# A retention block and two fused MLPs in float32: order of one chunk load, pacing of weight loads, and place of one pair's block sums

## The chip, the cores and the metric

The kernel runs on one core of one Trainium2 chip. Five engines of that core take part: TensorE (PE, with its weight loads on PEld), VectorE (DVE), ScalarE (ACT), and SyncE (SP), whose queue issues nearly all transfers; GpSimd is idle. The metric is device time in microseconds, the median of several executions.

## The reference

```
scores = q @ k.T / sqrt(64);  ret = scores * gamma_h ** (i - j) for i >= j, else 0;  a = ret @ v
x  = a, heads side by side                     # 2304 tokens x 512 (4 sequences of 576, 8 heads of 64)
x1 = softplus(x @ moe_w_in)   @ moe_w_out      # 512 -> 2048 -> 512
y  = relu(x1 @ moe2_w_in)**2  @ moe2_w_out     # 512 -> 2048 -> 512
```

All of it is float32. The kernel splits each operand into a high and a low part (fp32r) and makes three products of them (high x high, high x low, low x high).

## The kernel before

**Retention.** Tokens are handled in chunks of 128 (two halves of 64), 18 in all. The first four come from tiles of their own. From chunk 4 on, a chunk's q, k, v and a second k lie in one of two slots of `ring`; `load_chunk(c)` fills a slot with two transfers of 512 KB on SP's queue, first q and k (line 397, `ring<-in_qk_t_dram`), then k and v (`ring<-in_kv_dram`). Chunks c-1 and c+1 use the same slot. `visit(c, s)` issues the small matmuls of a half: outputs of chunk c-1 (L474), scores of chunk c (L426, which read q and k), states (L451). Then `masked` (L436, DVE) empties the scores, and `rest()`, called later in the same step, scales the outputs into x (`scaled`, L497 or L505). For tokens from 1280 on, `scaled` also stores x to `x1d` (L500). After the visit with s = 1 `rest()` ended with `load_chunk(c + 1)`.

**First MLP, tiles.** The first 1280 tokens go in three tiles b = 0, 1, 2 of 512, 384, 384 tokens. Each has 16 steps f, one per block of 128 hidden units. A step issues `g1` (L558, 12 matmuls), ACT's softplus (L569), the visits that are due (`attend`), the split of the step before (`split_g`: ACT L576, DVE L577), `rest()`, and `g2` of the step before last (L592, 12 matmuls). Visits run until step f = 5 of the last tile, one a step. All of this is issued in the order in which it is written.

**Second layer's weights.** Weights come packed; `load_w` (L141 for w_in, L146 for w_out) brings one raw block of 512 KB into one of three `stage` buffers, and `words` joins it into a `ct` tile with two ACT operations (L170, L171) and one or two DVE operations (L176, L179). `split_s` and `split_o` join two such blocks, form block sums for a Strassen-like product, split them (ACT L232, DVE L233) and store them to `s2d` or `o2d` (L235). One such item takes nine calls of `pump_step`: four for the two joins and five for the sums and stores. `pace(goal)` calls `pump_step` at the end of a step until the goal is reached. In the tiles b = 1 and 2 a step also stores a quarter of one group of w_out to `wod` (L1577), for six groups that are to be overwritten and reloaded later (`reload`, L1122).

**First MLP, full block.** The other 1024 tokens go through `block_first` (Strassen-like products `full_product`, L1015, pair p of hidden blocks after pair) and `block_second` (L1148). Their operands are made in the last tile: `load_full` brings x back (L939, into `ring`), `sums_full` and `build_full` make `t1` (L969, L718), and for pair 0 `words_of_pair` (L979) and `make_s` (L987, L996, L718) make the weight side `s`. The second MLP (`second_phase`, L697, and `second_products`, L770) follows. From `block_first` on, the order of instructions is a planner's.

Of the kernel before, what the change touches and what calls it, by code (L numbers as in the profile page):

```python
# [16 lines left out]
P = 128  # L17
# [4 lines left out]
STAGES = 3  # L22
# [13 lines left out]
A11, A12, S2, S4, S3, S1, A22 = range(7)  # L36
PRODUCTS = (A11, S2, A12, S3, S1, A22, S4)
T_SLOTS = 8
T_GROUPS = (0, 2, 3, 4)
S_GROUP = 5  # L40
G_GROUP = 1
ITEM = 9
SIGNED = 9
S_SLOTS = 10
# [10 lines left out]
def kernel(  # L55
# [70 lines left out]
    KH = KD // 2  # L126

    x1d = dram.tile([2 * FULL // CN, P, KD * CN], F32, name="x1d")
    wod = dram.tile([S_GROUP + 1, P, 4 * DM], F32, name="wod")
    s2d = dram.tile([NP, 7, P, 2, KH * P], F32, name="s2d")  # L130
    o2d = dram.tile([NP, 7, P, 2, KH * P], F32, name="o2d")

# [14 lines left out]
        staged[kind, f] = t  # L147

    last_softplus = []

    def words(t, ct):

        y, up, low = t.bitcast(F32)[:, :, 1], t[:, :, 1], t[:, :, 0]  # L160
        halves = t.bitcast(U16).rearrange("p a (b two) -> p a b two", two=2)
        half = halves[:, :, 0, 1]
        signed = n_split[0] - n_one > SIGNED
        if signed:
            with tc.issue_after(last_softplus[0].ins):
                nc.scalar.activation(
                    out=y, in_=y, func=AF.Prelu, scale=2.0**-112, alpha=-(2.0**32)
                )
        else:
            nc.scalar.activation(out=y, in_=y, func=AF.Copy, scale=2.0**-112)  # L170
        nc.scalar.activation(  # L171
            out=low, in_=half, func=AF.Identity, bias=round_up, scale=7.0 / 65535
        )
        yield
        if not signed:
            nc.vector.scalar_tensor_tensor(  # L176
                out=y, in0=y, scalar=-(2.0**32), in1=y, op0=ALU.mult, op1=ALU.max
            )
        nc.vector.scalar_tensor_tensor(  # L179
            out=ct, in0=up, scalar=3, in1=low,  # L180
            op0=ALU.logical_shift_left, op1=ALU.bitwise_or,
        )
        yield

    def new_ct(dtype=U32):
# [54 lines left out]
    def split_s(p):  # L240

        cts = []
        for f in (p, p + NP):
            t = staged.pop(("wi", f))
            cts.append(new_ct())
            yield from words(t, cts[-1])
        pump_load(n_used[0] + STAGES)
        top, bot = (ct.bitcast(F32) for ct in cts)
        a11, a12 = top[:, :KH * P], top[:, KH * P:]
        a21, a22 = bot[:, :KH * P], bot[:, KH * P:]  # L250
        store_s(s2d, p, A11, top)
        yield
        store_s(s2d, p, A22, a22)
        yield

        nc.vector.tensor_tensor(out=a22, in0=a21, in1=a22, op=ALU.add)
        nc.vector.tensor_tensor(out=a21, in0=a11, in1=a21, op=ALU.subtract)
        nc.vector.tensor_tensor(out=a11, in0=a22, in1=a11, op=ALU.subtract)
        nc.vector.tensor_tensor(out=a12, in0=a12, in1=a11, op=ALU.subtract)
        yield  # L260
        store_s(s2d, p, S3, bot)
        yield
        store_s(s2d, p, S2, top)
        yield True


    def split_o(p):

        cts = []
        for f in (p, p + NP):  # L270
            t = staged.pop(("wo", f))
            cts.append(new_ct())
            yield from words(t, cts[-1])
        pump_load(n_used[0] + STAGES)
        top, bot = (ct.bitcast(F32) for ct in cts)
        a11, a21 = top[:, :KH * P], top[:, KH * P:]
        a12, a22 = bot[:, :KH * P], bot[:, KH * P:]
        store_s(o2d, p, 0, a11)
        yield
        store_s(o2d, p, 1, bot)  # L280
        yield

        nc.vector.tensor_tensor(out=a22, in0=a21, in1=a22, op=ALU.add)
        nc.vector.tensor_tensor(out=a21, in0=a11, in1=a21, op=ALU.subtract)
        nc.vector.tensor_tensor(out=a11, in0=a22, in1=a11, op=ALU.subtract)
        nc.vector.tensor_tensor(out=a12, in0=a12, in1=a11, op=ALU.subtract)
        yield
        store_s(o2d, p, 3, top)
        yield
        store_s(o2d, p, 5, bot)  # L290
        yield True
# [30 lines left out]
    def pump_step():  # L322

        if not splitting:
            m = n_split[0]
            if m == len(items):
                return
            count, make, args = items[m]
            pump_load(n_used[0] + count)
            splitting.append(make(*args))  # L330
            n_split[0] += 1
            n_used[0] += count
        if next(splitting[0]):
            splitting.clear()
            pump_load(n_used[0] + STAGES)

    def pump(count):

# [607 lines left out]
    def sums_full(k):  # L946

        r00, r01, r10, r11 = (full_raw(i, j) for i in range(2) for j in range(2))
        if k == 1:
            full["t2"] = group_tile(G_GROUP, [P, 4 * DM], F32, "t2")[:, :KB]  # L950
            minus(r00, r01, r00)
            minus(full["t2"], r11, r00)
        elif k == 3:
            minus(r10, r10, full["t2"])
            minus(r01, r11, r01)
# [168 lines left out]
    def block_second():  # L1124

        accs = [
            [ps_acc.tile([P, 512], F32, tag="at", name="acc") for _ in range(KD)],
            [
                pool.tile([P, 512], F32, tag=tag, name="acc")
                for pool, tag in (  # L1130
                    (ps_h, f"h{n_h[0] % 2}"), (ps_h, f"h{(n_h[0] + 1) % 2}"),
                    (ps_at, "at"), (ps_st, "st"),
                )
            ],
        ]
        for g in (0, 4, 5):
            reload(g)
        split_full(2)
        for u, (f, half) in enumerate(f_units):
            at, second = divmod(u, 2)  # L1140
            begin, end = at == 0, at == KF - 1
            split_full(u + AHEAD)
            h, l = f_pairs.pop(u)
            wh, wl = of_group(f)
            for j in range(KD):
                c = slice(j * P, (j + 1) * P)
                for m, (a, x) in enumerate(((wh, h), (wh, l), (wl, h))):
                    nc.tensor.matmul(  # L1148
                        accs[half][j], lhsT=a[:, c], rhs=x,
                        start=(begin and m == 0), stop=(end and m == 2),  # L1150
                    )
            if end:
                for j in range(KD):
                    t0 = BLOCK + half * FULL
                    drain_one(j, accs[half][j], x2d[j, :, t0:t0 + FULL], FULL)
            pace(PACE[3] + (PACE[4] - PACE[3]) * (u + 1) // 26)
            if second:
                if at == 5:
                    for g in (1, 2, 3):
                        reload(g)  # L1160
                if at == 8:
                    mem["s"] = xs.tile([P, 4, 2, KH * P], F32R, tag="xr", name="sring")
                    load_s(4)
                m = {7: 0, 8: 1, 10: 2, 11: 3, 12: 4, 13: 5, 14: 6}.get(at)
                if m is not None:
                    build_t(m)
        assert n_split[0] == len(items) and not splitting
# [312 lines left out]
    def visit(c, s):  # L1480
# [11 lines left out]
        if s == 0:  # L1492
            if old:
                then.update(at_rounds((0, states(c - 1, 1))))
            rounds(first, then)
        else:
            if new:
                then.update(at_rounds((0, states(c, 0))))
            rounds(then, first)
        if new:  # L1500
            masked(c, 1 - s, pb)

        def rest():
            if s == 0 and old:
                next_state(c - 1, 1)
            elif s and new:
                next_state(c, 0)
            if old:
                scaled(c - 1, s, po)
            if s == 0:  # L1510
                scale_v(c)
            else:
                if old:
                    del chunk[c - 1]
                    load_chunk(c + 1)
        return rest


# [21 lines left out]
            return lambda: drain(t0, n)  # L1540

    n_taken = [0]

    def step(j):
        b, f = steps[j]
# [23 lines left out]
            load_chunk(last + 1)  # L1569
        if done:  # L1570
            done()
        if b:
            pace(PACE[b - 1] + (PACE[b] - PACE[b - 1]) * max(f - 1, 0) // (KF - 2))
        g, i = divmod((b - 1) * KF + f, 4)
        if 0 <= g <= S_GROUP:
            words_out = wo_group[g].rearrange("p a b n -> p (a b) n").bitcast(F32)
            nc.sync.dma_start(out=wod[g][:, i * DM:(i + 1) * DM], in_=words_out[:, i])  # L1577
        if b == last_b:
# [3 lines left out]
                build_full(BUILD_AT.index(f))  # L1582
            if f in SUMS_AT:
                sums_full(SUMS_AT[f])
            if f == KF - 3:
                words_of_pair(0)
            if f == KF - 2:
                made = make_s(0)
                next(made)
                next(made)  # L1590
                full["s0"] = made
            if ends:
                for _ in range(3):
                    next(full["s0"])

    def run(j0, j1):
        for j in range(j0, j1):
# [87 lines left out]
```

## Time and profile before

| | |
|---|---|
| median of 3 runs | 844.51 us (844.33 to 844.76) |
| profiled execution | 842.79 us, span 841.0 us |
| PE busy | 809.7 us (96%) |
| PEld busy | 717.8 us (85%) |
| DVE busy | 654.0 us (78%) |
| ACT busy | 402.3 us (48%) |
| DMA | 201.97 MB, mean 240 GB/s |
| mean granted TensorE clock | 0.991 of full speed |

The span runs from the first to the last instruction of the profiled execution. The share of PE is high, but matmuls are pipelined and their ends are modelled, so what counts is where PE sat idle, and behind what. "Clock" is the TensorE clock that was granted as a share of 2.4 GHz; 0.5 is the level of 1.2 GHz.

### The profile page before, as it was taken

To read this page: it belongs to the slowest core of one execution; us is meant where nothing else is said; L and a number is where in the kernel's file an instruction comes from. 1 tells how busy PE (TensorE), PEld (TensorE's weight loads), DVE (VectorE), ACT (ScalarE), POOL (GpSimd) and SP (SyncE) were. 2 spreads that over 40 slices of the span, in tenths; PEclk is the share of its full clock that TensorE was granted. 3 is DMA by queue.
4 is the path that set the end of the run, shared out by engine and by line. 5 is a ranking of instruction groups with operands and counts; after the bars stand their busy time and mean duration, and the time that the engine had idled before them with its cause. 6 is when DMAs were issued, how large, how long until landed. Compare 5 with 4: busy or idle time off the path is not lost.

```text
span 841.0 us, 16335 instructions
## 1 busy us (share of the span) xinstructions
PE 809.7 (96%) x5909; PEld 717.8 (85%) x5909; DVE 654.0 (78%) x1255; ACT 402.3 (48%) x781; POOL 0.2 (0%) x4
## 2 busy tenths in 40 slices
PE   8899999978799989999999999999999999999998
PEld 5678889967689978888888899988999988999887
DVE  4899885654635788996778788989698997787876
ACT  3888773543333665565657521355321554111453
POOL 0000000000000000000000000000000000000000
PEclk9999999999989999999999999999999999999999
DMA  9757664787766854335899988898988788878785
GB/s 243 261 179 235 216 213 178 252 287 245 235 204 197 248 178 148 101 113 200 303 327 281 311 289 252 251 302 270 301 257 251 247 262 281 289 251 248 254 273 172
DMA packets 129747, 201.97 MB, mean 240 GB/s; under 512 B 11010, under 2 KB 73090, under 8 KB 128898
## 3 DMA queue, kind: packets, MB, share of 16 engines
q1 hardware_dynamic: 129504, 200.85, 74.7%
q8 instruction: 47, 0.77, 0.4%
q14 instruction: 32, 0.26, 0.1%
q10 hardware_dynamic: 164, 0.09, 0.1%
HBM read 153.71 MB, written 47.19 MB: 239 GB/s over the span
## 4 chain that ended last, share of the span: by engine, by line
PE 84%; DMA 8%; DVE 4%; ACT 2%; SPq 1%; issue 1%; DVEq 0%; ACTq 0%
PE acc L592 11%; PE acc L1148 10%; PE ph L558 9%; PE py L697 9%; PE py L770 9%; PE px L697 6%; PE pz L770 6%; PE px L770 6%; PE pz L697 6%; PE py L1015 3%; DMA ring<-in_qk_t_dram 3%; PE pz L1015 2%; PE px L1015 2%; PE po L474 1%; PE pb L426 1%; DMA qk<-in_qk_t_dram 1%
## 5 line engine op out<-in xcount | busy, mean ns | idle before, releaser
L592 PE MATMUL acc<-gh,wo 128*128 128x384 f32 (+1 forms) x384 | 119.3, 372 | 0.0
L697 PE MATMUL py<-t,sring 128*128 128x384 f32 x432 | 88.3, 338 | 0.8 <-DVE uring L901 0.8
L558 PE MATMUL ph<-xh,wi 128*128 128x384 f32 (+1 forms) x376 | 79.8, 353 | 2.8 <-DVE ring L436 1.4
L592 PEld LDWEIGHTS acc<-gh,wo 128*128 128x128 f32 x384 | 73.6, 195 | 7.5 <-ACT gh L576 0.4
L697 PEld LDWEIGHTS py<-t,sring 128*128 128x128 f32 x432 | 74.8, 188 | 3.4 <-DVE uring L901 1.6
L558 PEld LDWEIGHTS ph<-xh,wi 128*128 128x128 f32 x376 | 67.3, 188 | 8.6 <-issue 1.7
L592 PE MATMUL acc<-gl,wo 128*128 128x384 f32 (+1 forms) x192 | 70.3, 366 | 1.3 <-DVE gl L577 1.3
L718 DVE TENSOR_TENSOR gring<-g,gring 128x384 fp32r<-128x384 f32 (+1 forms) x100 | 57.4, 578 | 14.1 <-ACT gring L750 9.2
L750 ACT CAST gh<-g 128x384 fp32r<-128x384 f32 x84 | 43.1, 514 | 47.5 <-PE px L770 16.7
L718 DVE TENSOR_TENSOR gl<-g,gh 128x384 fp32r<-128x384 f32 (+1 forms) x100 | 57.7, 578 | 10.1 <-ACT gh L750 8.0
L750 ACT CAST gring<-g 128x384 fp32r<-128x384 f32 x84 | 43.1, 514 | 40.3 <-PE py L770 16.4
L436 DVE TENSOR_TENSOR ring<-pb,cst 64x256 f32<-64x256 f32 x56 | 23.6, 421 | 48.1 <-PE pb L426 32.8
L697 PE MATMUL pz<-t,sring 128*128 128x384 f32 x288 | 58.9, 334 | 0.0
L697 PE MATMUL px<-t,sring 128*128 128x384 f32 x288 | 58.3, 335 | 0.0
L569 ACT ACTIVATE e<-ph 128x384 f32<-128x384 f32 (+1 forms) x48 | 25.2, 525 | 69.0 <-PE ph L558 68.7
L718 DVE TENSOR_TENSOR g<-g 128x384 f32<-128x384 f32 x96 | 52.6, 555 | 1.4
L897 ACT COPY uring<-px 128x384 f32<-128x384 f32 x24 | 11.6, 481 | 87.6 <-PE px L697 87.6
L232 ACT CAST ct<-ct 128x512 fp32r<-128x512 f32 (+1 forms) x64 | 35.9, 565 | 34.2 <-DMA s2d<-ct 16.9
L697 PEld LDWEIGHTS px<-t,sring 128*128 128x128 f32 x288 | 50.5, 188 | 0.6 <-ACT uring L897 0.5
L697 PEld LDWEIGHTS pz<-t,sring 128*128 128x128 f32 x288 | 50.8, 188 | 0.0
L233 DVE TENSOR_TENSOR ct<-ct 128x512 fp32r<-128x512 f32 (+1 forms) x64 | 39.2, 621 | 13.8 <-ACT ct L232 9.3
L1148 PE MATMUL acc<-gring,wo 128*128 128x512 f32 x192 | 44.8, 389 | 0.0
(155 smaller groups left out, 1753.4 us busy)
## 6 DMA issues: line engine op xcount, KB each, us to landing
sring<-s2d SPq DMA_DIRECT2D x168, 256.0 KB, 3.2
sring<-o2d SPq DMA_DIRECT2D x168, 256.0 KB, 3.4
wi_raw<-in_moe_w_in_dram SPq DMA_DIRECT2D x32, 512.0 KB, 5.9
wo_raw<-in_moe_w_out_dram SPq DMA_DIRECT2D x32, 512.0 KB, 4.4
s2d<-ct SPq DMA_DIRECT2D x48, 256.0 KB, 2.8
o2d<-ct SPq DMA_DIRECT2D x48, 256.0 KB, 3.2
ring<-in_qk_t_dram SPq DMA_DIRECT2D x14, 512.0 KB, 5.2
ring<-in_kv_dram SPq DMA_DIRECT2D x14, 512.0 KB, 6.1
```

What stands on the lines that cost most here:

```text
L232: nc.scalar.copy(h, src)
L233: nc.vector.tensor_tensor(out=l, in0=src, in1=h, op=ALU.subtract)
L436: nc.vector.tensor_tensor(out=chunk[c][rows, 1, i * HH:(i + 1) * HH], in0=pb[of], in1=mask[of], op=ALU.mult)
L558: nc.tensor.matmul(ph[:, :n], lhsT=a, rhs=x, start=(j == 0), stop=(j == len(todo) - 1))
L569: nc.scalar.activation(out=g, in_=hps.pop(key)[:, :n], func=AF.Softplus)
L592: nc.tensor.matmul(acc[j][:, :n], lhsT=a, rhs=x, start=(begin and m == 0), stop=(end and m == 2))
L697: nc.tensor.matmul(ps, lhsT=a, rhs=x, start=(first and m == 0), stop=(m == len(todo) - 1), skip_group_check=True,)
L718: nc.vector.tensor_tensor(out=out, in0=a, in1=b, op=ALU.subtract)
L750: nc.scalar.copy(h, src)
L770: nc.tensor.matmul(blocks[m][:, :cols], lhsT=a[:, c], rhs=x, start=(first and p == n == 0), stop=(p == NP - 1 and n == len(todo) - 1), ski ...
L1015: nc.tensor.matmul(ps, lhsT=a, rhs=x, start=(first and m == 0), stop=(m == len(todo) - 1), skip_group_check=True,)
L1148: nc.tensor.matmul(accs[half][j], lhsT=a[:, c], rhs=x, start=(begin and m == 0), stop=(end and m == 2),)
```

## The change

Four things change, and a few names follow them.

1. In `visit`, `load_chunk(c + 1)` is issued right behind the visit's matmuls, where it stood behind the scaling and, for late tokens, behind the store of x.
2. `pump_load` is called after every `pump_step` for at most one block, up to three blocks ahead of the blocks joined so far (`n_joined`). Before, it was called once an item, when both of its blocks had been joined, and then issued two.
3. In the last tile, pacing begins at f = 0 (it began at f = 2) and leaves out f = 8 and f = 11, the steps of `sums_full`.
4. For pair 0, `words_of_pair` and the block sums of `make_s` move to f = 7 (from f = 13 and 14), and its four splits to f = 12 to 15, one a step (from one at f = 14 and three at f = 15). For this `s` takes the place of weight group 0, with `t2` before it, group 1 takes the first `t1`, and the first output `g` of `block_first` takes group 5. So group 5 is reloaded with groups 1 to 3 in the middle of `block_second`, and no longer with groups 0 and 4 at its start.

```diff
-T_GROUPS = (0, 2, 3, 4)
-S_GROUP = 5
-G_GROUP = 1
+T_GROUPS = (1, 2, 3, 4)
+S_GROUP = 0
+G_GROUP = 5
...
+    n_joined = [0]
...
             op0=ALU.logical_shift_left, op1=ALU.bitwise_or,
         )
+        n_joined[0] += 1
         yield
...
             yield from words(t, cts[-1])
-        pump_load(n_used[0] + STAGES)
         top, bot = (ct.bitcast(F32) for ct in cts)
...
         if next(splitting[0]):
             splitting.clear()
-            pump_load(n_used[0] + STAGES)
+        pump_load(min(n_load[0] + 1, n_joined[0] + STAGES))
...
-            full["t2"] = group_tile(G_GROUP, [P, 4 * DM], F32, "t2")[:, :KB]
+            full["t2"] = group_tile(S_GROUP, [P, 4 * DM], F32, "t2")[:, :KB]
...
-        for g in (0, 4, 5):
+        for g in (0, 4):
             reload(g)
...
                 if at == 5:
-                    for g in (1, 2, 3):
+                    for g in (5, 1, 2, 3):
                         reload(g)
...
             rounds(then, first)
+        if s and old:
+            load_chunk(c + 1)
         if new:
             masked(c, 1 - s, pb)
...
             if s == 0:
                 scale_v(c)
-            else:
-                if old:
-                    del chunk[c - 1]
-                    load_chunk(c + 1)
+            elif old:
+                del chunk[c - 1]
...
-        if b:
-            pace(PACE[b - 1] + (PACE[b] - PACE[b - 1]) * max(f - 1, 0) // (KF - 2))
+        if b == 1:
+            pace(PACE[0] + (PACE[1] - PACE[0]) * max(f - 1, 0) // (KF - 2))
+        elif b and f not in (8, 11):
+            n_paced[0] += 1
+            pace(PACE[1] + (PACE[2] - PACE[1]) * n_paced[0] // (KF - 2))
...
-            if f == KF - 3:
+            if f == RAW_AT + 1:
                 words_of_pair(0)
-            if f == KF - 2:
-                made = make_s(0)
-                next(made)
-                next(made)
-                full["s0"] = made
-            if ends:
-                for _ in range(3):
-                    next(full["s0"])
+                full["s0"] = make_s(0)
+                next(full["s0"])
+            if f >= KF - 4:
+                next(full["s0"])
```

## Rows read from the trace of the kernel before

**Rows 1.** Waits of PE over the whole span: us in total, times, longest

```profile
PE pb L426 <- DMA ring<-in_qk_t_dram: 15.1, 6, 4.2
PE py L1015 <- ACT s L996: 2.8, 1, 2.8
PE ph L558 <- DVE ring L436: 1.4, 1, 1.4
```

**Rows 2.** Timeline of PE, rows with idle time before them (in brackets, with releaser)

```profile
170.73 0.27 PE L426 MATMUL pb<-ring 64*64 64x64 f32 x2 [1.07 <-DMA ring<-in_qk_t_dram]
...
186.19 0.27 PE L426 MATMUL pb<-ring 64*64 64x64 f32 x2 [2.56 <-DMA ring<-in_qk_t_dram]
...
201.36 0.27 PE L426 MATMUL pb<-ring 64*64 64x64 f32 x2 [3.94 <-DMA ring<-in_qk_t_dram]
215.60 0.27 PE L426 MATMUL pb<-ring 64*64 64x64 f32 x2 [1.48 <-DMA ring<-in_qk_t_dram]
...
231.09 0.37 PE L426 MATMUL pb<-ring 64*64 64x64 f32 x2 [4.23 <-DMA ring<-in_qk_t_dram]
246.27 0.27 PE L426 MATMUL pb<-ring 64*64 64x64 f32 x2 [1.78 <-DMA ring<-in_qk_t_dram]
...
306.69 0.44 PE L592 MATMUL acc<-gl,wo 128*128 128x384 f32 x1 [0.90 <-DVE gl L577]
```

**Rows 3.** Stretches: busy us of PE, PEld, DVE, ACT, POOL; clock, DMA share, GB/s

```profile
144.00:232.00 88.00, 73.33 (x1090) 68.27 (x1089) 52.53 (x108) 37.20 (x82) 0.00 (x0) 0.96 0.80 258
232.00:264.00 32.00, 30.22 (x385) 28.38 (x383) 14.28 (x29) 10.86 (x24) 0.00 (x0) 0.94 0.53 171
264.00:302.00 38.00, 37.80 (x219) 37.45 (x218) 26.62 (x41) 20.52 (x37) 0.00 (x0) 1.00 0.77 229
```

**Rows 4.** Timeline of PE: first matmul of g2 behind a visit

```profile
142.66 0.45 PE L592 MATMUL acc<-gh,wo 128*128 128x384 f32 x1
...
176.82 0.45 PE L592 MATMUL acc<-gh,wo 128*128 128x384 f32 x1
...
208.96 0.45 PE L592 MATMUL acc<-gh,wo 128*128 128x384 f32 x1
```

**Rows 5.** Timeline of SP's queue: start, time of issue

```profile
142.81 0.33 SPq L397 DMA_DIRECT2D ring<-in_qk_t_dram  x1
...
180.12 0.49 SPq L1577 DMA_DIRECT2D wod<-wo  x1
...
426.85 0.75 SPq L1122 DMA_DIRECT2D wo<-wod  x1
```

**Rows 6.** Chain that ended last, in order of time: start, us

```profile
170.09 8.13 DMA s2d<-ct
...
181.93 4.22 DMA ring<-in_qk_t_dram
...
186.87 2.28 PE acc L592 x12
...
194.64 6.58 DMA ring<-in_qk_t_dram
...
202.14 3.73 PE acc L592 x12
...
211.44 4.12 DMA ring<-in_qk_t_dram
...
232.21 4.01 PE acc L592 x12
...
314.25 3.59 PE acc L592 x12
...
395.25 87.04 PE acc L1148 x384
```

**Rows 7.** DVE's groups by line and shape, 264 to 316: busy, mean ns

```profile
L718 DVE TENSOR_TENSOR y<-y 128x256 f32<-128x256 f32 x3 | 1.3, 423 | 0.1
...
L979 DVE TENSOR_TENSOR y<-wi,wi 128x512 f32<-128x512 f32 x1 | 0.7, 685 | 0.0
```

**Rows 8.** The line of the reloads of weight groups (`wo<-wod`, six transfers)

```profile
DMA to landing us min/median/max: 4.7/7.2/8.8
```

More of the change, by code (lines that the diff above doesn't have):

```diff
@@ L128 @@
     x1d = dram.tile([2 * FULL // CN, P, KD * CN], F32, name="x1d")
-    wod = dram.tile([S_GROUP + 1, P, 4 * DM], F32, name="wod")
+    wod = dram.tile([G_GROUP + 1, P, 4 * DM], F32, name="wod")
     s2d = dram.tile([NP, 7, P, 2, KH * P], F32, name="s2d")
@@ L334, in pump_step @@
             splitting.clear()
-            pump_load(n_used[0] + STAGES)
+        pump_load(min(n_load[0] + 1, n_joined[0] + STAGES))
     def pump(count):
@@ L1542 @@
     n_taken = [0]
+    n_paced = [0]
     def step(j):
@@ L1571, in step @@
             done()
-        if b:
-            pace(PACE[b - 1] + (PACE[b] - PACE[b - 1]) * max(f - 1, 0) // (KF - 2))
+        if b == 1:
[3 more added lines that the diff above has]
+            pace(PACE[1] + (PACE[2] - PACE[1]) * n_paced[0] // (KF - 2))
         g, i = divmod((b - 1) * KF + f, 4)
-        if 0 <= g <= S_GROUP:
+        if 0 <= g <= G_GROUP:
             words_out = wo_group[g].rearrange("p a b n -> p (a b) n").bitcast(F32)
```

## The prediction

> **What bounds the kernel now.** PE is busy for 96% of the span, so I read first for what it waited. The table of PE's waits names one thing above all others: scores matmuls that waited for a chunk's q and k, 15.1 us in six waits. Behind it come one wait of 2.8 us for pair 0's weight sums and one of 1.4 us for DVE's masking [rows 1]. PE's timeline puts the six waits between 170 and 247 us, at every second step, with 1.07, 2.56, 3.94, 1.48, 4.23 and 1.78 us [rows 2]. The second half of the span has no such idle time, so what is gained early stays gained as long as nothing new stalls there.
>
> The stretches show why the chunks are late. From 144 to 232 us PE is busy for 73.3 of 88 us, while the transfers run at 258 GB/s with the DMA engines 80% busy [rows 3]. A queue that full has little idle time, and a load that enters it late lands late. The chain of waits has q and k landing 4.22, 6.58 and 4.12 us after their issue, and one store of weight sums 8.13 us after [rows 6].
>
> The sum below is made against the profiled execution, 842.79 us (span 841.0 and 1.8 around it). The median of the runs is 1.72 us higher, and I take the sum off the median.
>
> **Part 1, the load ahead of x's store.** How soon could a load leave? In the step where no store of x stood in front, PE went over to g2 at 142.66 [rows 4] and the load left at 142.81 [rows 5], 0.15 us later. The fourth late load could so have left at 208.96 + 0.15 = 209.11 [rows 4]. It left at 211.44 [rows 6], behind DVE's masking, split and scaling and the store of x. It gains 2.33 us. The first, third, fourth and sixth are of this kind. Their waits allow 1.07 + 2.33 + 1.48 + 1.78 = 6.66 us [rows 2].
>
> The second load could leave at 176.97 by its matmuls, but SP's queue is in order and was still issuing the step before's stores: that of `wod` began at 180.12 and took 0.49 [rows 5]. The load would leave at about 180.66 and left at 181.93 [rows 6], so it gains 1.27. I take the same for the fifth. Together 6.66 + 2.54 = 9.2 us; 5.9 us of waits stay. Everything passed is unharmed: the store of x needs no early landing, since x is read back only at f = 6 of the last tile. The load waits for PE alone, and what is queued behind it on SP is that store.
>
> Below this, an earlier load could land no earlier if the transfers in front of it set its landing: bound 0. Above, all 15.1 us could go.
>
> **Part 2, single loads.** Before, two blocks (1 MB) left back to back when an item's second join was done, among chunk loads and sum stores. Now the first leaves three pump steps sooner, in b = 1 about one step of the tile. At 258 / 0.80 = 322 GB/s a block is 1.6 us of queue [rows 3]. Where a pair stood ahead of a store or a chunk load, that goes, and the chunk load ahead of the store leaves 2.3 us sooner: the store that landed after 8.13 us [rows 6] should land some 3.9 us sooner. ACT's next split waits for that buffer, DVE's masking waits behind it, and so PE's 1.4 us [rows 1]. I take 1.0 of 1.4.
>
> For the 5.9 us left of part 1 I take nothing, though 1.6 us less queue would cover most. The reason: 258 GB/s for 88 us is 22.7 MB, which needs 70.6 us at 322 GB/s. PE has 73.3 us of work there, some of it at half clock. When the idle time goes, the queue must run near full, and full queues make waits of their own. Bounds 0 and 5.9.
>
> **The clock.** Behind the two longest waits the 12 matmuls of g2 took 3.73 and 4.01 us, against 2.28 in other steps [rows 6]: the granted clock fell to its lower level. The waits of 2.56 us and less were not followed by that. With the third wait down to 1.6 us and the fifth to 3.0 both losses should go: 1.45 + 1.73 = 3.2 us. Bounds 0 and 3.2.
>
> **Part 3, pair 0's sums sooner.** PE waited 2.8 us for the first `s` [rows 1], and the g2 behind it took 3.59 us, 1.3 over 2.28 [rows 6]. In the new order `s` is complete at f = 15. The two word additions (0.685 each [rows 7]) also leave the DVE queue just ahead of the `gl` for which PE waited 0.90 [rows 2]. Bounds 0 and 5.0; I take 4.0, for DVE still builds two operands in that place.
>
> The moved work costs: at f = 7 two additions of 0.685 and four sums of 0.42, 3.05 us; at f = 12 to 15 one 0.42 on DVE and a copy on ACT each [rows 7]. In 264 to 302 us DVE is busy 26.6 of 38 us and ACT 20.5 [rows 3], and pacing leaves out the two steps of the large sums, so DVE reaches some 31.4 of 38. A split may be late by a part of a step, and g2 uses it a step later. I cost it at nothing; without that cover it is what DVE is behind, up to 2 us. The pump steps that come two tile steps sooner fall into 232 to 264 us, where DVE is busy 14.3 of 32 us and the DMA share is 0.53 [rows 3]: nothing.
>
> **Part 4, group 5 reloaded late.** The one late reload before left at 426.85 [rows 5] and reloads land within 8.8 us [rows 8]. Group 5 would be there at 435.65. It is needed at the ninth of sixteen blocks, 395.25 + 87.04 x 8/16 = 438.77 [rows 6]. Nothing, with 3.1 us to spare. Groups 1 to 3 come later still.
>
> **Sum.** 9.2 + 1.0 + 3.2 + 4.0 = 17.4 us. 844.5 - 17.4 = 827.1 us.
>
> **The rivals.** *The queue is the limit (chance 0.19).* A load that leaves sooner stands behind the same bytes. Then perhaps half of part 1 comes, 4.6 us, the clock loss after one of the long waits stays (1.6 of 3.2 gained), the 1.4 stays, and part 3 gives its 4.0: 10.2 us, 834.3 us. For it speaks the 6.58 us landing, against it the 4.12 us of the fourth load in the same stretch [rows 6].
>
> *All waits go (0.14).* With blocks spread evenly the loads land in 4.2 us or so [rows 6]. A load has from g2's start to the next scores, and 142.81 shows one that caused no wait at all [rows 5]. Then 15.1 + 1.4 + 3.2 + 5.0 = 24.7 us go: 819.8 us. The Trainium skill (DMA: Bandwidth & Descriptors, Anatomy of one DMA) fits 2.0 us plus bytes over 436 GB/s, an estimate of 3.2 us for such a load, though for GpSimd's queue. The rows of this stretch are all longer; by that rule no chunk load that leaves at the matmuls' end would be waited for.
>
> *Slower (0.05).* Group 5's reload now sits on PE's path in the middle of `block_second`. If the planner puts it behind other transfers, PE waits there. It eats the whole gain only when it lands 3.1 + 17.4 = 20.5 us later than reckoned, 29 us after issue against 8.8 at most seen [rows 8]; at 35 us the time is 850. Unlikely, but it is the one new wait on a full queue. A small stall of a few us there stays inside the range.
>
> *No effect (0.03).* If the landing of the chunks follows the weight stores alone and pair 0's wait only moves to the next operand, nothing is left: 844.
>
> **How the numbers follow.** My forecast has 0.59 and reaches by itself from 823 to 831. The range takes in the first two rivals' values: 819.5 to 836.5 us, with about 2 in 10 outside. Within 0.2% (1.7 us) is what cannot be told from no change. Faster by more: 0.59 + 0.19 + 0.14 = 0.92. Slower: 0.05. The same: 0.03.
>
> **What would show it.** In the changed profile chunk loads from 160 us on should leave within 0.2 us of the end of the visit's matmuls, or right behind SP's stores, and stand ahead of x's store. PE's waits for q and k should fall from 15.1 to about 6 us. The half-speed g2 at 202, 232 and 314 us should be gone, and so the wait of py for `s`. Weight loads should come singly. `block_first` should begin some 13 us sooner, and everything from there on keep its length. The prediction is wrong if q and k then land later after their issue by as much as they leave sooner, if ACT's splits hold masking back in new places, or if PE waits for group 5.

## The result, and the profile after

The changed kernel takes 830.44 us (median of 4 runs, 829.30 to 835.78) where the kernel before takes 844.42: a ratio of 0.9853, 95% interval 0.9807 to 0.9900. In a second comparison the same kernel came to 0.9884 (0.9852 to 0.9915). So it is 10 to 12 us faster, 14 by the first medians. The forecast was 827.1 us (819.5 to 836.5): right in sign and inside its range, but too hopeful, by 3 us against the first median and by 7 against the second ratio, which would make 834.6 us of 844.4. The runs of one kernel spread by up to 9 us, so a single profile says where time went, and the ratios say how much.

The waits of PE over the whole span of the changed kernel (us in total, times, longest) answer to [rows 1]:

```profile
PE pb L426 <- DMA ring<-in_qk_t_dram: 7.6, 4, 2.7
PE ph L558 <- DVE ring L436: 1.5, 1, 1.5
...
PE acc L592 <- DVE xo L602: 1.1, 1, 1.1
```

The wait for pair 0's `s` is gone and the waits for q and k are halved. The 1.5 us for the masking stands at another place than the 1.4 us before, and the wait for `xo`, the copy that drains an accumulator, is new. PE's timeline shows where they are (idle time before a row in brackets), beside [rows 2]:

```profile
170.45 0.27 PE L426 MATMUL pb<-ring 64*64 64x64 f32 x2 [1.00 <-DMA ring<-in_qk_t_dram]
...
183.67 0.27 PE L426 MATMUL pb<-ring 64*64 64x64 f32 x2 [1.96 <-DMA ring<-in_qk_t_dram]
196.87 0.37 PE L426 MATMUL pb<-ring 64*64 64x64 f32 x2 [1.95 <-DMA ring<-in_qk_t_dram]
...
223.22 0.27 PE L426 MATMUL pb<-ring 64*64 64x64 f32 x2 [2.72 <-DMA ring<-in_qk_t_dram]
239.28 0.44 PE L592 MATMUL acc<-gh,wo 128*128 128x384 f32 x1 [1.12 <-DVE xo L602]
241.59 2.90 PE L558 MATMUL ph<-xh,wi 128*128 128x384 f32 x8 [1.52 <-DVE ring L436]
```

The first wait, 1.07 us before, is still 1.00. The fourth and the sixth are gone, but where the sixth was, at the second step of the last tile, PE now stands behind the drain and then behind the masking. The chain that ended last (start, us) names the rest:

```profile
164.44 5.96 DMA ring<-in_qk_t_dram
...
178.43 5.20 DMA ring<-in_qk_t_dram
...
190.35 6.38 DMA ring<-in_qk_t_dram
...
197.99 3.33 PE acc L592 x12
...
217.63 5.54 DMA ring<-in_qk_t_dram
...
223.90 3.84 PE acc L592 x12
...
232.90 5.65 DMA x1d<-x
...
241.59 3.69 PE ph L558 x12
```

Three things are read here. The loads leave sooner, but the four on the chain take 5.2 to 6.4 us to land. Over the six loads in question, those that caused no wait included, landing took 3.5 to 6.4 us, 5.2 on average; in the kernel before it was 3.7 to 6.6 and 4.7 on average. Three groups of 12 matmuls still ran in part at the lower clock level: 3.33 and 3.84 us against 2.28, and a g1 of 3.69 against 2.08, with granted clocks of 0.67, 0.56 and 0.60 in these stretches. And a store of x (`x1d<-x`) is on the chain.

The stretches (busy us of PE, PEld, DVE, ACT, POOL; clock, DMA share, GB/s) beside [rows 3]: PE does more in the same 88 us, the DMA engines are busier, and the mean clock of these two stretches is the same or nearly so.

```profile
144.00:232.00 88.00, 80.23 (x1181) 75.08 (x1180) 55.18 (x115) 39.63 (x88) 0.00 (x0) 0.96 0.84 271
232.00:264.00 32.00, 29.36 (x323) 27.48 (x322) 16.90 (x34) 12.31 (x26) 0.00 (x0) 0.95 0.70 227
```

Profile against profile (828.6 us of span against 841.0), by the start of the same work: 0.6 us were gained by the g2 at 136.69 (before at 137.27), of which 0.5 stood already at 40.76 (before at 41.29), so the change hardly has a part in them; 6.0 us by the step that begins at 246.37, before at 252.41; 10.4 us by `block_second`, which begins at 384.88 against 395.25 [rows 6]. The last 2.0 us lie in the second MLP and are most likely chance: the stretch from its first to its second `px` of L770 took 117.6 us here, 119.8 before, and 119.2 in another profile of the changed kernel itself. Without these 0.6 and 2.0 us the 12.4 us between the two profiles are 9.8, as much as the second ratio gives.

### The profile page after: what moved, and what is told of

The parts are those of the page before. It is cut to its first block, busy times and chain, and to the rows that moved or that the text cites. A ratio compares the mean times of both kernels' runs of the same rounds, so it can differ in the third digit from the quotient of the medians.

```text
span 828.6 us, 16334 instructions
## 1 busy us (share of the span) xinstructions
PE 806.9 (97%) x5909; PEld 716.1 (86%) x5909; DVE 653.4 (79%) x1255; ACT 402.8 (49%) x781; POOL 0.2 (0%) x4
## 4 chain that ended last, share of the span: by engine, by line
PE 80%; DMA 10%; DVE 5%; ACT 2%; issue 1%; SPq 1%; DVEq 0%; ACTq 0%
PE acc L1148 10%; PE acc L592 9%; PE py L770 9%; PE py L697 9%; PE ph L558 9%; PE pz L770 6%; PE px L770 6%; PE pz L697 6%; PE px L697 6%; DMA ring<-in_qk_t_dram 3%; PE py L1015 3%; PE pz L1015 2%; PE px L1015 2%; DMA wi_raw<-in_moe_w_in_dram 2%; PE po L474 1%
```

## The experiments

Each is timed beside the kernel before on the same chip. First the parts, one at a time.

**The load's place alone.**

```diff
 # kernel before
             rounds(then, first)
+        if s and old:
+            load_chunk(c + 1)
         if new:
             masked(c, 1 - s, pb)
...
-            else:
-                if old:
-                    del chunk[c - 1]
-                    load_chunk(c + 1)
+            elif old:
+                del chunk[c - 1]
```

> The kernel before with one thing changed: the next chunk's load stands right behind the visit's matmuls; weights still load in pairs, pair 0's sums stay late. Theory A (the load's place is what pays in the tiles): PE's waits for q and k fall from 15.1 us to 6 to 8 us, pair 0's wait of 2.8 us stays, the time falls by 6 to 9 us (836 to 838). It also expects the stall at the last tile's second step (drain behind the x store that now follows 1 MB of chunk load), some 1 to 4 us. Theory B (the queue is the limit: behind a pair of weight blocks an earlier load lands no earlier): the waits stay above 11 us and the time falls by less than 3 us.

Measured: 835.26 us, ratio 0.9903 (0.9885 to 0.9921), 8 us faster. In its profile the waits for q and k are 8.9 us, the wait for `s` is the same 2.8, and PE waits 1.0 us for the drain. The gain is theory A's; the waits, at 8.9, lie a little above its 6 to 8. Theory B, with waits above 11 us and a gain under 3, does not hold.

**Single weight loads alone.**

```diff
 # kernel before
+        n_joined[0] += 1          # behind each join
...
-        pump_load(n_used[0] + STAGES)   # twice, behind both joins of an item
...
             splitting.clear()
-            pump_load(n_used[0] + STAGES)
+        pump_load(min(n_load[0] + 1, n_joined[0] + STAGES))
```

> The kernel before with one thing changed: the second layer's weight blocks load singly, each behind the join that frees a buffer. Theory A: little by itself, 0 to 2 us, the six waits for q and k stay at 12 to 16 us, as the loads still leave behind x's store. Theory B (pairs of blocks fill the queue, singles clear it): the long stores of weight sums land in under 5 us, the waits fall to 8 to 10 us and the time by 5 us or more. A third possibility: singles leave one tile step sooner, right ahead of a chunk load, and so cost as much as they give: the same to 2 us slower.

Measured: 842.21 us, ratio 0.9992 (0.9968 to 1.0015): no difference that shows. All six waits for q and k stay, 12.6 us in its profile.

**Pair 0's sums, the exchanged groups and the last tile's pacing alone.** The edit is parts 3 and 4 of the change on the kernel before.

> The kernel before with pair 0's sums moved to the eighth step of the last tile, the weight groups exchanged for it, and the new pacing in the last tile; chunk loads and weight loads as before. Theory A: PE's wait of 2.8 us for the first weight sum and the half-clock matmuls behind it go, 4 to 5 us faster (about 840), the waits for q and k unchanged at 15 us. Theory B (the wait only moves to the next operand that is still being built): under 1.5 us faster, and a new wait of PE in the first pair.

Measured: 838.24 us, ratio 0.9942 (0.9918 to 0.9967), 4.9 us faster. No wait of PE for `s` is left and no new one stands in the first pair. Theory A. The six waits for q and k are all there, 13.7 us. The run does not part the sums' place from the new pacing; that the gain is the sums' is argued from the wait that went.

The three ratios multiplied give 0.984; the change itself measured 0.9853 and 0.9884. The parts add up, within what these runs can tell. Undoing one part of the change tells the same from the other side.

**The changed kernel once more**, beside three of the variants below.

> The changed kernel once more, unaltered, beside the three variants of it that follow. All theories: 829 to 832 us, 0.983 to 0.988 of the kernel before.

Measured: 832.75 us, 0.9884 (0.9852 to 0.9915), just above the expected ratio.

**The change without its load move.** The first edit, taken back.

> The changed kernel with one part undone: the chunk load stands behind the scaling and x's store again. Theory A (the parts add up): what pair 0's sums and pacing (4.9 us) and singles (0.7 us) gave alone, 0.992 to 0.995 of the kernel before, about 837; waits for q and k 12 to 15 us, no wait for the drain. Theory B (singles need the early load, or the reverse): 841 or above.

Measured: 837.91 us, ratio 0.9933 (0.9907 to 0.9959); waits for q and k 14.1 us, none for the drain. Theory A.

**The change without single loads.** The second edit, taken back.

> The changed kernel with one part undone: the second layer's weight blocks load in pairs again, behind an item's second join. Theory A (the parts add up, and singles are worth what they gave alone, under 1 us): 0 to 1.5 us slower than the changed kernel. Theory B (singles pay only once the chunk loads stand at the matmuls' end, since then pairs are what is ahead of them): 2 to 4 us slower, waits for q and k 2 us or more above those of the changed kernel. Theory C (a single block leaves just ahead of a chunk load and delays it): 1 to 2 us faster.

Measured: 833.40 us, 0.9878 (0.9850 to 0.9906), the same as the changed kernel beside it. What single loads do is seen at the first chunk load. SP's queue of the changed kernel (this second profile of it) and PE at the next scores:

```profile
162.54 0.38 SPq L141 DMA_DIRECT2D wi_raw<-in_moe_w_in_dram  x1
162.98 0.50 SPq L1581 DMA_DIRECT2D wod<-wo  x1
164.25 0.33 SPq L397 DMA_DIRECT2D ring<-in_qk_t_dram  x1
...
171.00 0.27 PE L426 MATMUL pb<-ring 64*64 64x64 f32 x2 [1.74 <-DMA ring<-in_qk_t_dram]
```

With pairs, no block leaves before that load and PE does not wait there at all; it waits at the next one, behind the pair:

```profile
164.58 0.33 SPq L397 DMA_DIRECT2D ring<-in_qk_t_dram  x1
...
166.87 1.32 SPq L141 DMA_DIRECT2D wi_raw<-in_moe_w_in_dram  x2
...
179.09 1.63 PE L558 MATMUL ph<-xh,wi 128*128 128x384 f32 x8 [1.39 <-DVE ring L436]
184.55 0.37 PE L426 MATMUL pb<-ring 64*64 64x64 f32 x2 [2.42 <-DMA ring<-in_qk_t_dram]
```

So by these two profiles the single block that leaves 1.7 us ahead of the chunk load costs a wait there, and spares two waits that the pair causes a step later. That is theory A's number with theory C's mechanism inside it. How much each side is worth is not shown: in the first profile of the changed kernel PE waits at both places, 1.00 and 1.96 us.

**One visit with x's store first.** The drain's wait was the surprise. DVE's timeline in the changed kernel at that step:

```profile
232.79 0.55 DVE L602 COPY xo<-acc 128x384 f32<-128x384 f32 x1
238.67 0.56 DVE L602 COPY xo<-acc 128x384 f32<-128x384 f32 x1 [5.34 <-DMA x1d<-x]
239.15 0.68 DVE L177 SCALAR_TENSOR_TENSOR wi_raw<-wi_raw 128x512 f32<-128x512 f32 x1
239.86 0.69 DVE L180 SCALAR_TENSOR_TENSOR ct<-wi_raw 128x512 uint32<-128x512 uint32 x1
240.59 0.86 DVE L436 TENSOR_TENSOR ring<-pb,cst 64x256 f32<-64x256 f32 x2
```

The drain's odd copies use the same two tiles as x (tag "l"). The store that frees one now stands behind 1 MB of chunk load. The dependence could be read before the change: there DVE already waited at this place, for less time and with no wait of PE for the drain behind it.

```profile
243.67 0.56 DVE L602 COPY xo<-acc 128x384 f32<-128x384 f32 x1 [1.87 <-DMA x1d<-x]
```

Over all 16 stores of x in the changed kernel, times to landing:

```profile
DMA to landing us min/median/max: 1.7/3.9/7.3
```

Before, that line read 1.7/1.8/3.8. In the changed kernel DVE stands still for 5.3 us; the join of a weight block (1.4 us), which the new pacing puts into this step, follows, and only then the masking for which g1 waits.

```diff
 # changed kernel
-        if s and old:
+        if s and old and c + 1 != NPR - 1:
             load_chunk(c + 1)
...
             elif old:
                 del chunk[c - 1]
+                if c + 1 == NPR - 1:
+                    load_chunk(c + 1)
```

> The changed kernel, but in the one visit in whose step the second tile's accumulators are drained, the last chunk's load stands behind x's store again. Theory A (there the store of x lands late behind 1 MB of chunk load, the drain waits for its buffer, DVE's masking waits behind the drain, and PE for both): PE's waits of 1.1 us for the drained accumulator and 1.5 us for the masking go, the slow g1 after them too, and a wait for q and k of 0 to 2 us comes back; 2 to 4 us faster than the changed kernel. Theory B (the drain is late for other reasons, such as the pump steps that now lie in that step): the waits of 1.1 and 1.5 us stay and the time is the same.

Measured: 833.17 us, 0.9869 (0.9844 to 0.9893): no faster than the change, as far as these intervals can tell, and theory A's 2 to 4 us did not show. Its mechanism is seen in the profile all the same. Both waits and the slow g1 are gone, and a wait for q and k of 1.94 us stands there again. Against 4.2 us that would be a gain of some 2 us, too little to tell from chance here.

**Another buffer for the drain.** This keeps both.

```diff
 # changed kernel, drain_one
+        elif n == TILES[1][1]:
+            o = cvt.tile([P, 512], F32, tag="ct", name="xo")[:, :n]
+            nc.vector.tensor_copy(o, src[:, :n])
         else:
             o = ew.tile([P, 512], F32, tag="l", name="xo")[:, :n]
```

> The changed kernel with one buffer changed: the second tile's drain copies its odd accumulators into tiles of the pool of joined weights, where they shared two tiles with x. So no drain waits for x's store, while the chunk load stays ahead of that store. Theory A (the shared buffer alone couples the drain to x's store): PE's waits of 1.1 us for the drain and 1.5 us for the masking, and the slow g1 behind them, go without a wait for q and k in their place; 2 to 4 us faster than the changed kernel. Theory B: the drain now waits for a weight sum's store instead, or the next x does; the same time.

The condition holds for both tiles of 384 tokens, so the third tile's drain moves as well.

Measured: 826.71 us, 0.9819 (0.9787 to 0.9850), 6 us below the changed kernel beside it at 832.75. PE's waits from 130 to 330 us:

```profile
PE pb L426 <- DMA ring<-in_qk_t_dram: 9.6, 6, 2.4
PE acc L592 <- DVE gl L577: 0.5, 1, 0.5
PE py L1018 <- DVE u L1108: 0.5, 1, 0.5
```

Neither drain nor masking is waited for, and no wait stands at that step. Theory A, at more than its upper figure; the intervals of the two ratios (the changed kernel's begins at 0.9852) just fail to meet. Not all of the 6 us is the buffer's as far as the traces show. The waits for q and k are 9.6 us here and 8.0 in the changed kernel's profile beside it, so PE waits only about 1 us less in all. By these two profiles the rest is the clock: the granted clock was 0.98 from 144 to 232 us and 1.00 from 232 to 264, against 0.92 and 0.95 in that profile. The first of these stretches lies ahead of the drain, and no run shows that the buffer acts on it.

**The load's place and the drain's buffer, on the kernel before.**

> The kernel before with two things changed: the chunk load stands at the end of the visit's matmuls, and the second tile's drain copies its odd accumulators into tiles of the pool of joined weights. Theory A (the load's place by itself was worth some 12 us, of which the drain's wait for x's store took 4): 829 to 832 us, 0.984 to 0.988 of the kernel before; no wait of PE for the drain. Theory B (the gain of the other buffer needs singles or the new pacing): 834 to 836, as with the load's place alone.

Measured: 834.05 us, 0.9882 (0.9853 to 0.9912), against 0.9903 with the load's place alone: theory B's range, though the interval takes in most of theory A's. No wait for the drain is left; in another step its profile has a wait of 2.6 us for masking. In the old pacing no join stands in the drain's step. The profile of the load's place alone shows the same hold-up of DVE, but with the masking right behind it, and PE lost 1.0 and 0.2 us there:

```profile
240.91 0.56 DVE L602 COPY xo<-acc 128x384 f32<-128x384 f32 x1 [5.23 <-DMA x1d<-x]
241.50 0.86 DVE L436 TENSOR_TENSOR ring<-pb,cst 64x256 f32<-64x256 f32 x2
```

So in the profiles the shared buffer cost about 1 us by itself, and 4.2 us in the change (1.12 + 1.52 + 1.61 for the slow g1), where the earlier pacing puts a join between the drain and the masking.

**Less weight work in the second tile.** This asks whether the other waits come from the full queue.

```diff
 # changed kernel
-    PACE = (0, 4 * ITEM, 7 * ITEM, SIGNED * ITEM, 2 * NP * ITEM)
+    PACE = (0, 27, 7 * ITEM, SIGNED * ITEM, 2 * NP * ITEM)
```

> The changed kernel with 27 pump steps in the second tile and 36 in the third, where it has 36 and 27: a quarter of the second layer's block loads and sum stores of the second tile moves to the third, whose later steps have no chunk loads. Nothing is left out. Theory A (the rest of the waits for q and k comes from a transfer queue that is nearly full in the second tile): the DMA share from 144 to 225 us falls to about 0.72, the waits fall from about 8 to 10 us to 2 to 5, the time by 3 to 6 us (825 to 827). Theory B (the waits come from SP's in-order queue and from landing times that no load shortens): the waits stay above 7 us, the time is within 1.5 us of the changed kernel. Theory C: the added work stalls the third tile (DVE is behind at its middle), new waits of PE for gl of 2 us or more, no gain.

Measured: 827.97 us, 0.9822 (0.9796 to 0.9849), 4.8 us below the changed kernel beside it. The DMA share from 144 to 225 us fell only to 0.80 from 0.86, and the waits did fall. A new one came at the middle of the third tile:

```profile
PE pb L426 <- DMA ring<-in_qk_t_dram: 5.3, 4, 1.8
PE acc L592 <- DVE gl L577: 2.6, 2, 2.3
```

Theory C's wait came, and a time 1 us above theory A's. A's figure for the DMA share missed, and so its step from share to wait is not shown, only that with less weight work there PE waits less. The edit moves that work's operations on ACT and DVE along with its transfers, so which of them counted stays open.

**Both, with 27 and with 31 pump steps.**

> The changed kernel with both improvements: the drain's other buffer, and 27 pump steps in the second tile with 36 in the third. Theory A (two separate causes, the shared buffer and the nearly full queue): gains add, 820 to 824 us. Theory B (both shorten the same stretch of the third tile's start): 825 to 827, as with either alone. The wait of 2.3 us for gl at the third tile's middle is expected to stay.

Measured: 826.80 us, 0.9811 (0.9776 to 0.9847): no better than either alone (theory B), with the wait for gl still there (2.2 us).

> As the run before, with 31 pump steps in the second tile and 32 in the third. Theory A: the wait for gl at the third tile's middle shrinks to under 1 us, the waits for q and k come out between 5 and 9 us; 820 to 825 us, within 2 us of the run with 27. Theory B (only clearing the second tile's queue counts): 2 to 4 us slower than with 27.

Measured: 823.26 us, 0.9760 (0.9731 to 0.9790), the fastest kernel here, 20 us below the kernel before. The wait for gl is down to 1.2, not under 1, and its six runs lie within 3.1 us. It is 3.5 us faster than the run with 27, more than expected; the two intervals overlap by a little. PE's waits from 130 to 330 us:

```profile
PE pb L426 <- DMA ring<-in_qk_t_dram: 5.7, 4, 1.9
PE ph L558 <- DVE ring L436: 1.6, 1, 1.6
PE acc L592 <- DVE gl L577: 1.2, 1, 1.2
```

## Why the prediction was right, and where it was off

*What bounds the kernel.* Right: the waits for q and k and for `s` were time to be had, and what was gained by `block_second` was kept to the end.

*Part 1, 9.2 us.* The loads left as reckoned: at 164.44 and 204.12 right with the matmuls' end, at 178.43, 190.35 and 217.63 right behind SP's stores. What was mis-sized is how much of that lands. I let the landing time stay. The first load left at 164.44 instead of 166.94, 2.5 us sooner, and landed 5.96 us after its issue, where before it took:

```profile
DMA to landing us min/median/max: 3.7/3.7/3.7
```

So its wait went from 1.07 only to 1.00. The second wait came down to 1.96 and not to 1.3, the third to 1.95 and not to 1.6. In all the waits fell by 7.5 us, 15.1 to 7.6, and not by 9.2. With its share of the clock and the price of the drain this part gave 8 us alone (0.9903), and 4 to 7 us inside the change (0.9933 without it).

*"Everything passed is unharmed: the store of x needs no early landing."* This step failed. I followed what reads x's data and not what waits for x's tile. The drain shares it, and DVE stood 5.3 us for it. In the change this cost 4.2 us in the profile; giving the drain another tile brought 6, part of it in the clock of steps ahead of the drain.

*Part 2, 1.0 us, and nothing for the left-over waits.* The masking's old wait did go in the changed profile, but single loads show no gain: 0.9992 alone, 0.9878 against 0.9884 when undone. I named the full queue as the reason for taking nothing. The run with 27 steps fits that and does not show it, since it moves other work too.

*The clock, 3.2 us.* Wrong in its step. In the profile two slow groups of g2 became two others, which cost 1.05 and 1.56 us, and a slow g1 was added. I had read from two waits of about 4 us against four of 2.6 and less that only long waits are followed by the lower level. The last section shows that this does not hold. On average the clock did rise: 0.990 over ten runs of the kernel before, 0.993 over six of the changed kernel beside them. So something of this term came, part of it with the slow g2 of part 3.

*Part 3, 4.0 us.* Right: 4.9 us alone with the new pacing, 4.4 in the profile from 246.37 to `block_second`, with no wait moved to the next operand. The additions at f = 7 cost little: PE waits 0.59 us for gl at 279.03, where in the kernel before it waited 0.90 at 306.69 [rows 2]. The sign I gave, `block_first` some 13 us sooner, was wrong: it began at 301.88 instead of 308.73, 6.9 us sooner, and the wait for `s` lies behind that start.

*Part 4, nothing.* Right: the late reload left at 416.56, PE shows no wait in `block_second`.

The sum was 17.4 and the change gave 10 to 14, so it lies between the forecast and the first rival (the queue as limit, 10.2 us and 834.3), and by the second ratio at that rival. The first load behaved as that rival says. That the first median came out within 3 us of the forecast is in part luck: the 0.6 and 2.0 us that are not the change's stood in for a part of what the drain and the clock took away. The rival in which all waits go is out: 7.6 us of them stay. The Trainium skill (DMA: Bandwidth & Descriptors, Anatomy of one DMA) gives, for GpSimd's queue, an estimate of 3.2 us for such a load; the six loads here, on SP's queue, took 3.5 to 6.4.

## What to carry to other kernels

When a transfer is moved ahead of a store, follow the store's source tile as well as its data: who next takes that buffer, and what stands behind that taker on its engine. In a stretch where the DMA engines are 80% busy, do not count on a load landing as much sooner as it leaves: here the first gained 2.5 us in leaving and 0.2 in landing. Moving a quarter of the weight work out of that stretch gave another 4.8 us. A gain read from waits should be taken without the clock, unless the trace shows more than two cases.

## What the runs showed of the hardware

The lower clock level does not follow from the length of the wait in front of it alone. In the first profile of the changed kernel the waits of 1.96 and 1.95 us (183.67 and 196.87, shown above) were followed by these stretches, in the order of [rows 3]; the clock is the third number from the end:

```profile
184.28:186.50 2.22, 2.22 (x17) 2.22 (x14) 2.05 (x5) 0.03 (x1) 0.00 (x0) 1.00 1.04 367
197.99:201.32 3.33, 3.33 (x13) 3.33 (x14) 3.25 (x7) 1.12 (x3) 0.00 (x0) 0.67 0.51 179
```

So of two waits of the same length one was followed by full speed and one was not. In the profile of pair 0's sums alone, a wait of 3.27 us was followed by full speed:

```profile
232.59 0.27 PE L426 MATMUL pb<-ring 64*64 64x64 f32 x2 [3.27 <-DMA ring<-in_qk_t_dram]
...
233.20:235.40 2.20, 2.20 (x17) 2.20 (x14) 2.04 (x5) 0.27 (x1) 0.00 (x0) 1.00 1.05 372
```

In the second profile of the changed kernel a wait of 1.74 us (shown above) was followed by this, on the chain:

```profile
171.68 3.85 PE acc L592 x12
...
198.06 3.33 PE acc L592 x12
...
225.60 4.14 PE acc L592 x12
```

That execution had a mean granted clock of 0.990 and took 833.88 us, the first profile of the same kernel 0.994 and 830.39. The profiles of the two kernels with the drain in other tiles and 36 or 31 steps had 0.998. Of 17 runs of the kernel before, the fastest (839.29 us) had 0.992 and the slowest (848.55) 0.983. So the spread between runs of one kernel goes with the clock, and a part of what small waits cost may be this.
